# A decode attention block whose first 57 pairs run in a device loop of 19 rounds

## The chip, the cores and the metric

The kernel runs on one core of one Trainium2 chip. The metric is the device time of one execution in microseconds (us). A profile of one execution gives the instructions of each engine and the transfers of the DMA queues: PE does the matmuls (PEld their weight loads), DVE the vector work, ACT the activations, POOL next to nothing here, and SP issues nearly all transfers.

## What is computed

One token of each of two sequences goes through a pre-norm attention block with a cached history of 8192 keys and values for 32 heads of 128, and then through a dense block with a squared ReLU. All is float32. Cut to what matters:

```python
# x (2,1,512); k_cache, v_cache (2,32,8192,128); wq (512,4096); wo (4096,512)
q = (layernorm(x) @ wq).reshape(2, 1, 32, 128).transpose(0, 2, 1, 3)
scores = einsum("bhqd,bhkd->bhqk", q, k_cache) * 128 ** -0.5
o = einsum("bhqk,bhkd->bhqd", softmax(scores), v_cache)
h = x + o.transpose(0, 2, 1, 3).reshape(2, 1, 4096) @ wo
r = relu(layernorm(h) @ w1 + b1)          # w1 (512,1792)
out = h + (r * r) @ w2 + b2               # w2 (1792,512)
```

Keys and values are 537 MB, and the weights come to 24 MB more; each byte is used once.

## The kernel before

The work is cut into 64 pairs of a head and a sequence. A pair's keys and values lie side by side in one block of 128 partitions x 16384 numbers (8.39 MB), keys in the first half, values in the second. The tile `ring` has three such blocks, its slots. Pair i lies in slot (i + 1) modulo 3, except for the last two.

**Head.** SP loads the query weights into slot 0 (L69) and pairs 0 and 1 into slots 1 and 2 (L70, L71). The layer norm and the query projection run while these arrive (L127 to L146). L148 scales the 64 query columns and spreads each over 32 columns, which gives the tile QR. Pair 2 is loaded into slot 0 once the query weights have been read (L149).

**A pair.** `scores` (L157) does 32 matmuls of 128x512 on a score tile of four banks, of which the pool `psum` has two (line L162), and DVE takes the negated maximum of each row (L164). `exponentials` (L167) lets ACT do the exponential in place and add up the rows (L169). `weighted` (L171), four times a pair, lets DVE multiply the values by the exponentials and add up, in place in the slot (L174). The results of a pair go into column i of NM, LS and AC.

**Order of the work.** The loop at L236 over pairs 0 to 62 is a Python loop: its instructions stand one after the other in the program. After each pair SP gets the load of pair i + 3 into the slot just freed (L242, L58). SP's loads are one queue in order, and each waits until DVE is done with its slot. From pair 59 on, the output weights, halves of the last pairs and the two `group` steps (merging rows and projecting) are put in between (L243 to L258). After the loop come the weights of the dense block, the last pair and the tail (L260 to L341).

Of the kernel before, what the change touches and what calls it, by code (L numbers as in the profile page):

```python
# [8 lines left out]
F32 = mybir.dt.float32  # L9
AF = mybir.ActivationFunctionType  # L10
ALU = mybir.AluOpType
AX = mybir.AxisListType

B, H, SK, DH, D, F = 2, 32, 8192, 128, 512, 1792
P = 128
NQ = 4
CS = SK // NQ
NH = DH // 32
# [3 lines left out]
BH = H * B  # L22
ROW = 16384
HALF = ROW // 2
SLOTS = 3
BLK = 512
GROUPS = [(0, 16), (16, 31), (31, 32)]
W2_PIECES = [4, 4, 3, 2, 1]
EPS = 1e-5
SCALE = DH ** -0.5  # L30

# [2 lines left out]
def attention_block_kernel(ctx: ExitStack, tc: tile.TileContext, small, kvd, wqd, wod, w1d, w2d, out):  # L34
    nc = tc.nc
    consts = ctx.enter_context(tc.tile_pool(name="consts", bufs=1))
# [6 lines left out]
    def slot(i):  # L43
        return ring[:, (i + 1) % SLOTS if i < BH - 2 else i - BH + 3]

    def keys(i):
        return slot(i)[:, :HALF].rearrange("p (j c) -> p j c", j=NQ)

    def values(i):
        return slot(i)[:, HALF:].rearrange("p (e c) -> p e c", e=NH)  # L50
# [6 lines left out]
    def load_kv(i):  # L57
        nc.sync.dma_start(slot(i), kvd[i])  # L58

    def load_wo(a, b):  # L60
        nc.sync.dma_start(WO[:, a:b], wod[:, a:b])
# [14 lines left out]
    eps_t = consts.tile([P, 1], F32, name="eps_t")  # L76
    nc.vector.memset(eps_t, EPS)
    zero = consts.tile([P, 1], F32, name="zero")
# [11 lines left out]
    def banks(name="s"):  # L90
        t = psum.tile([P, NQ * BLK], F32, name=name)
        return t, [t[:, k * BLK : (k + 1) * BLK] for k in range(NQ)]

    def clear(ap, n):
        return nc.scalar.activation(ap, zero.to_broadcast([P, n]), AF.Copy)  # L95
# [27 lines left out]
    _, bk = banks()  # L123
# [11 lines left out]
    for k in range(2):  # L135
        for d in range(DB):
            for j in range(NQ):
                n = k * NQ + j
# [4 lines left out]
    for k in range(2):  # L143
        for m in range(NQ):
            at = k * BLK + m * DH
            nc.tensor.matmul(turned[:, k, m], big[:, at : at + DH], quads[:, :, :B], start=True, stop=True)  # L146
    QR = consts.tile([P, BH, 32], F32, name="QR")
    nc.vector.tensor_scalar(QR, bk[2][:, :BH, None].to_broadcast([P, BH, 32]), SCALE, None, op0=ALU.mult)  # L148
    load_kv(2)  # L149


    NM = consts.tile([P, BH], F32, name="NM")
    LS = consts.tile([P, BH], F32, name="LS")
    AC = consts.tile([P, BH, NH], F32, name="AC")
    OT = consts.tile([P, BH], F32, name="OT")

    def scores(i):  # L157

        s, bk = banks()
        for n in range(CS // BLK):  # L160
            for j in range(NQ):
                nc.tensor.matmul(bk[n][32 * j : 32 * j + 32, :], QR[:, i, :], keys(i)[:, j, n * BLK : (n + 1) * BLK],  # L162
                                 start=True, stop=True)
        nc.vector.tensor_reduce(NM[:, i : i + 1], s, axis=AX.X, op=ALU.max, negate=True)  # L164
        return s

    def exponentials(i, s):  # L167

        nc.scalar.activation(s, s, AF.Exp, bias=NM[:, i : i + 1], scale=1.0, accum_out=LS[:, i : i + 1])  # L169

    def weighted(i, s, e, lo, hi, acc, by=1.0):  # L171

        v = values(i)[:, e, lo:hi]
        return nc.vector.scalar_tensor_tensor(v, v, by, s[:, lo:hi], op0=ALU.mult, op1=ALU.mult, accum_out=acc)  # L174
# [44 lines left out]
    last = BH - 1  # L219
    g_at = [(a * B, b * B) for a, b in GROUPS]  # L220

    def group(n, project_now):

        a, b = g_at[n]
        _, bk = banks()
        w, rl = weigh(a, b, bk[0], bk[1])
        join(a, b, w, rl, bk[2])
        if project_now:
            clear(bk[3], D)
            add_rows(project(*GROUPS[n], bk[3]), bk[0])  # L230

    def load_half(i, half):
        cut = slice(half * HALF, (half + 1) * HALF)
        nc.sync.dma_start(slot(i)[:, cut], kvd[i][:, cut])

    for i in range(last):  # L236
        s = scores(i)
        exponentials(i, s)
        for e in range(NH):
            weighted(i, s, e, 0, CS, AC[:, i, e : e + 1])  # L240
        if i + 3 < last - 1:
            load_kv(i + 3)  # L242
        if i == last - 4:  # L243
            load_wo(0, H // 2)
        if i == last - 3:
            load_half(last - 1, 0)
            load_half(last - 1, 1)
            group(0, True)
        if i == last - 2:
            load_half(last, 0)  # L250
            load_wo(H // 2, H)
            for e in range(NH):
                n = 2 if e == NH - 1 else 1
                for k in range(n):
                    lo, hi = k * CS // n, (k + 1) * CS // n
                    at = HALF + e * CS
                    nc.sync.dma_start(values(last)[:, e, lo:hi], kvd[last][:, at + lo : at + hi])
            group(1, False)  # L258
# [3 lines left out]
    at = 0  # L262
    for n in W2_PIECES:
        nc.sync.dma_start(W2[:, at : at + n], w2d[:, at : at + n])
        at += n
    sl = scores(last)
    _, (hp, sums, y, o) = banks()
    y, o = y[:, :FQ], o[:, :P]
    clear(hp, D)
    clear(y, FQ)  # L270
    with tc.issue_after(clear(o, P).ins):
        exponentials(last, sl)
    a, b = g_at[2]
    w, rl = weigh(a, b, sums[:, :64], sums[:, 64:128])
    nc.scalar.activation(warm, w[:, 0:1], AF.Sqrt)
# [21 lines left out]
    for e in range(NH + 1):  # L297
        at = 32 * min(e, NH - 1)
# [73 lines left out]
```

## Time and profile before

| | before |
|---|---|
| median of 2 runs | 1309.41 us (1309.08 to 1309.75) |
| profiled execution | 1310.04 us, its span 1308.3 us |
| instructions | 6011 |
| PE busy | 417.7 us (32%) |
| DVE busy | 728.9 us (56%) |
| ACT busy | 145.0 us (11%) |
| moved by DMA | 561.44 MB, mean 429 GB/s |
| mean granted PE clock | 0.643 |

The span is the time from the first to the last instruction. "Busy" counts the time in which an engine executes, not its waits. A group of instructions is named by line, engine, operation and output<-input. In the chain that ended last, the profile goes back from the last instruction, at each step to what released it. In the waits, each line says which engine and line waited for what, how long in total, how often, and the longest.

### The profile page before, as it was taken

Reading aid. Unit: us, or ns where it says so; the run is one execution under the profiler, and the core shown is the slowest. Engines: PE = TensorE matmul, PEld = TensorE weight load, DVE = VectorE, ACT = ScalarE, POOL = GpSimd, SP = SyncE. Lnnn points to the kernel's source line nnn. Section 1 sums busy time; section 2 is a strip of 40 time slices with the busy share of each in tenths; the row PEclk is TensorE's granted clock in tenths of the full one; section 3 lists DMA queues with packets and bytes.
Section 4 is the critical chain, followed back from the end, with each engine's and each line's share of the span. In section 5 each row is a group of like instructions: output and inputs, shape, how many; then the busy total and the mean of one; then the engine's idle time right before and its main releaser. Section 6 shows DMA issues by size and latency. Waiting matters only on the chain.

```text
span 1308.3 us, 6011 instructions
## 1 busy us (share of the span) xinstructions
PE 417.7 (32%) x2438; PEld 114.7 (9%) x2438; DVE 728.9 (56%) x626; ACT 145.0 (11%) x152; POOL 0.7 (0%) x6
## 2 busy tenths in 40 slices
PE   2423223323323323322322332332332332332446
PEld 0100000000000000000000000000000000000113
DVE  0464665564565565565566466556456556556553
ACT  1111011011011011011101101101101101101111
POOL 0000000000000000000000000000000000000000
PEclk9666667566656666666656666756665665665766
DMA  9999999999999999999999999999999999999997
GB/s 417 417 447 425 439 433 431 441 425 443 425 439 423 441 429 435 433 435 432 433 431 435 430 437 431 435 431 433 431 437 429 437 429 437 428 439 429 426 426 313
DMA packets 12122, 561.44 MB, mean 429 GB/s; under 512 B 1472, under 2 KB 1600, under 8 KB 2752
## 3 DMA queue, kind: packets, MB, share of 16 engines
q1 hardware_dynamic: 11952, 561.06, 99.3%
q8 instruction: 19, 0.31, 0.1%
q14 instruction: 7, 0.06, 0.0%
q10 hardware_dynamic: 144, 0.01, 0.0%
HBM read 561.00 MB, written 0.07 MB: 429 GB/s over the span
## 4 chain that ended last, share of the span: by engine, by line
DMA 62%; DVE 20%; PE 12%; ACT 4%; another core or an unknown queue 1%; issue 1%; SPq 0%; ACTq 0%
DMA ring<-in_kvd 62%; DVE ring L174 16%; PE s L162 11%; DVE NM L164 4%; ACT s L169 4%; PE s L315 0%; PE s L337 0%; PE s L308 0%; DVE yT L329 0%; PE s L189 0%; PE s L321 0%; PE s L327 0%; SPq L58 0%; PE s L326 0%
## 5 line engine op out<-in xcount | busy, mean ns | idle before, releaser
L162 PE MATMUL s<-ring,QR 128*32 128x512 f32 x2048 | 373.1, 895 | 827.1 <-DMA ring<-in_kvd 718.9
L174 DVE SCALAR_TENSOR_TENSOR ring<-ring,s 128x2048 f32<-128x2048 f32 x252 | 561.5, 2284 | 133.6 <-ACT s L169 133.6
L164 DVE TENSOR_REDUCE NM<-s 128x1 f32<-128x2048 f32 x64 | 146.6, 2291 | 383.4 <-PE s L162 383.4
L169 ACT ACTIVATE s<-s,NM 128x2048 f32<-128x2048 f32 x64 | 124.3, 1942 | 1072.5 <-DVE NM L164 1072.5
L162 PEld LDWEIGHTS s<-ring,QR 128*32 128x32 f32 x2048 | 93.3, 156 | 1104.4 <-issue 1100.9
L174 DVE DVE_READ_ACCUMULATOR ring<-ring,s 128x1 f32 x252 | 20.9, 83 | 0.0
L99 DVE TENSOR_REDUCE part<-sm 128x2 f32<-128x8 f32 x1 | 0.2, 160 | 21.9 <-DMA sm<-in_small 21.9
L169 ACT ACTIVATION_READ_ACCUMULATOR s<-s,NM 128x1 f32 x64 | 12.3, 193 | 0.0
L139 PE MATMUL s<-ring,xn 128*2 128x512 f32 x64 | 9.5, 749 | 1.5 <-ACT rstd L117 0.8
L174 DVE SCALAR_TENSOR_TENSOR ring<-ring,w,s 128x2048 f32<-128x2048 f32 (+1 forms) x5 | 9.6, 1916 | 0.6 <-DMA ring<-in_kvd 0.4
L207 PE MATMUL s<-ring,OT 128*2 128x512 f32 x62 | 8.5, 682 | 3.8 <-DMA ring<-in_wod 3.5
L148 DVE TENSOR_SCALAR QR<-s 128x2048 f32<-128x2048 f32 x1 | 2.3, 2291 | 12.4 <-PE s L146 12.4
L104 PE MATMUL s<-part,ones_d 128*128 128x2 f32 x2 | 0.6, 348 | 23.2 <-DVE hT L132 23.2
L189 PE MATMUL s<-lw,pick_all 128*128 128x32 f32 (+2 forms) x6 | 1.9, 393 | 14.9 <-DVE lw L188 14.9
L315 PE MATMUL s<-ring,xc 128*2 128x448 f32 x32 | 6.3, 942 | 0.6 <-ACT rstd L117 0.4
L181 PE MATMUL s<-NM,pick 128*128 128x32 f32 (+2 forms) x24 | 4.0, 309 | 7.1 <-DVE hT L217 4.6
L95 ACT ACTIVATE s<-zero 128x512 f32<-128x512 f32 (+2 forms) x6 | 3.2, 538 | 19.8 <-DVE OT L201 10.7
L337 PE MATMUL s<-ring,a 128*2 128x128 f32 x112 | 4.7, 348 | 1.5 <-DVE a L334 1.5
L181 PEld LDWEIGHTS s<-NM,pick 128*128 128x128 f32 x24 | 3.7, 236 | 8.9 <-issue 8.9
L117 ACT ACTIVATE rstd<-s,eps_t 128x2 f32<-128x2 f32 x2 | 0.5, 262 | 32.1 <-PE s L128 20.0
L337 PEld LDWEIGHTS s<-ring,a 128*2 128x2 f32 x112 | 3.3, 107 | 3.1 <-DVE a L334 2.0
L340 DVE COPY res<-s 128x128 f32<-128x128 f32 x1 | 0.3, 292 | 4.9 <-PE s L337 4.9
(74 smaller groups left out, 45.3 us busy)
## 6 DMA issues: line engine op xcount, KB each, us to landing
ring<-in_kvd SPq DMA_DIRECT2D x3, 4096.0 KB, 32.4
ring<-in_wod SPq DMA_DIRECT2D x2, 4096.0 KB, 41.8
ring<-in_w1d SPq DMA_DIRECT2D x4, 896.0 KB, 20.3
ring<-in_kvd SPq DMA_DIRECT2D x3, 1024.0 KB, 38.2
ring<-in_w2d SPq DMA_DIRECT2D x2, 1024.0 KB, 16.2
ring<-in_kvd SPq DMA_DIRECT2D x2, 512.0 KB, 38.0
ring<-in_kvd SPq DMA_DIRECT2D x62, 38.8
ring<-in_w2d SPq DMA_DIRECT2D x1, 768.0 KB, 16.8
```

Of the source, the lines that this page charges most:

```text
L95: return nc.scalar.activation(ap, zero.to_broadcast([P, n]), AF.Copy)
L139: nc.tensor.matmul(bk[k][32 * j : 32 * j + B, :], xn[:, d, :], WQ[:, d, n * BLK : (n + 1) * BLK], start=(d == 0), stop=(d == DB - 1))
L148: nc.vector.tensor_scalar(QR, bk[2][:, :BH, None].to_broadcast([P, BH, 32]), SCALE, None, op0=ALU.mult)
L162: nc.tensor.matmul(bk[n][32 * j : 32 * j + 32, :], QR[:, i, :], keys(i)[:, j, n * BLK : (n + 1) * BLK], start=True, stop=True)
L164: nc.vector.tensor_reduce(NM[:, i : i + 1], s, axis=AX.X, op=ALU.max, negate=True)
L169: nc.scalar.activation(s, s, AF.Exp, bias=NM[:, i : i + 1], scale=1.0, accum_out=LS[:, i : i + 1])
L174: return nc.vector.scalar_tensor_tensor(v, v, by, s[:, lo:hi], op0=ALU.mult, op1=ALU.mult, accum_out=acc)
L181: nc.tensor.matmul(pn[:, j], pick[:, j, :], NM[:, a:b], start=True, stop=True)
L189: nc.tensor.matmul(pl[:, :nb], pick_all, lw, start=True, stop=True)
L207: nc.tensor.matmul(hp[32 * j : 32 * j + B, :], OT[:, h * B : (h + 1) * B], WO[:, h, :], start=(h - h0 < NQ), stop=(h1 - h <= NQ))
L315: mm = nc.tensor.matmul(y[32 * j : 32 * j + B, :], xc[:, d, :], W1[:, d, j * FQ : (j + 1) * FQ], start=(d == 0), stop=(d == DB - 1))
L337: nc.tensor.matmul(o[32 * j : 32 * j + B, :], a2[:, m, :], W2[:, m, j * P : (j + 1) * P], start=False, stop=(m == FB - 1))
```

## The change

Pairs 0 to 56 are worked on in a loop on the device, `tc.For_i` from 0 to 57 in steps of 3. The body does three pairs, each followed by the load of the pair three further on; the load's source address is taken from the loop's register, its slot is fixed. `iteration_sync="reg_based"` is the way in which rounds are kept in order: waits in the body compare with registers that go up in every round. `head_align_engines` puts the start of the body at the start of a block of code for all five engines, and `hint_engines=()` gives no hints for the branch back.

In the body the queries and results are in small tiles with fixed addresses (q3, nm3, ls3, ac3). DVE spreads the next three query columns into q3 after the third pair's maximum, and copies the three results into NM, LS and AC at the end of the round. QT holds the scaled queries without the spread, and QR is left for the last seven pairs. Pairs 57 to 62 and what follows stay as they were, but for the new arguments of `scores` and `exponentials`.

```diff
+LOOPED = 57
...
-    QR = consts.tile([P, BH, 32], F32, name="QR")
-    nc.vector.tensor_scalar(QR, bk[2][:, :BH, None].to_broadcast([P, BH, 32]), SCALE, None, op0=ALU.mult)
+    QT = consts.tile([P, BH], F32, name="QT")
+    nc.vector.tensor_scalar(QT, bk[2][:, :BH], SCALE, None, op0=ALU.mult)
+    QR = consts.tile([P, BH - LOOPED, 32], F32, name="QR")
+    nc.vector.tensor_copy(QR, QT[:, LOOPED:, None].to_broadcast([P, BH - LOOPED, 32]))
     load_kv(2)
...
-    def scores(i):
+    def scores(i, q, nm):
...
-    def exponentials(i, s):
+    def exponentials(s, nm, ls):
...
-    for i in range(last):
-        s = scores(i)
-        exponentials(i, s)
+    q3 = consts.tile([P, SLOTS, 32], F32, name="q3")
+    nm3 = consts.tile([P, SLOTS], F32, name="nm3")
+    ls3 = consts.tile([P, SLOTS], F32, name="ls3")
+    ac3 = consts.tile([P, SLOTS, NH], F32, name="ac3")
+
+    def spread(at):
+        nc.vector.tensor_scalar(q3, QT[:, at, None].to_broadcast([P, SLOTS, 32]), 1.0, None, op0=ALU.mult)
+
+    spread(slice(0, SLOTS))
+    engines = (nc.tensor.engine, nc.vector.engine, nc.scalar.engine, nc.gpsimd.engine, nc.sync.engine)
+    with tc.For_i(0, LOOPED, SLOTS, hint_engines=(), head_align_engines=engines, iteration_sync="reg_based") as i0:
+        now = bass.ds(i0, SLOTS)
+        for u in range(SLOTS):
+            nm, ls = nm3[:, u : u + 1], ls3[:, u : u + 1]
+            s = scores(u, q3[:, u, :], nm)
+            if u == SLOTS - 1:
+                spread(bass.ds(i0 + SLOTS, SLOTS))
+            exponentials(s, nm, ls)
+            for e in range(NH):
+                weighted(u, s, e, 0, CS, ac3[:, u, e : e + 1])
+            nc.sync.dma_start(slot(u), kvd[bass.ds(i0 + (SLOTS + u), 1)].rearrange("o p c -> p (o c)"))
+        for all_, three in ((NM, nm3), (LS, ls3), (AC, ac3)):
+            nc.vector.tensor_scalar(all_[:, now], three, 1.0, None, op0=ALU.mult)
+
+    for i in range(LOOPED, last):
+        nm, ls = NM[:, i : i + 1], LS[:, i : i + 1]
+        s = scores(i, QR[:, i - LOOPED, :], nm)
+        exponentials(s, nm, ls)
         for e in range(NH):
             weighted(i, s, e, 0, CS, AC[:, i, e : e + 1])
```

More of the change, by code (lines that the diff above doesn't have):

```diff
@@ L161, in scores @@
             for j in range(NQ):
-                nc.tensor.matmul(bk[n][32 * j : 32 * j + 32, :], QR[:, i, :], keys(i)[:, j, n * BLK : (n + 1) * BLK],
+                nc.tensor.matmul(bk[n][32 * j : 32 * j + 32, :], q, keys(i)[:, j, n * BLK : (n + 1) * BLK],
                                  start=True, stop=True)
-        nc.vector.tensor_reduce(NM[:, i : i + 1], s, axis=AX.X, op=ALU.max, negate=True)
+        nc.vector.tensor_reduce(nm, s, axis=AX.X, op=ALU.max, negate=True)
         return s
-    def exponentials(i, s):
-        nc.scalar.activation(s, s, AF.Exp, bias=NM[:, i : i + 1], scale=1.0, accum_out=LS[:, i : i + 1])
+    def exponentials(s, nm, ls):
+        nc.scalar.activation(s, s, AF.Exp, bias=nm, scale=1.0, accum_out=ls)
     def weighted(i, s, e, lo, hi, acc, by=1.0):
@@ L265, in attention_block_kernel @@
         at += n
-    sl = scores(last)
+    sl = scores(last, QR[:, last - LOOPED, :], NM[:, last : last + 1])
     _, (hp, sums, y, o) = banks()
@@ L271, in attention_block_kernel @@
     with tc.issue_after(clear(o, P).ins):
-        exponentials(last, sl)
+        exponentials(sl, NM[:, last : last + 1], LS[:, last : last + 1])
     a, b = g_at[2]
```

## The prediction

> **What bounds the kernel now.** I read the utilisation slices first, then the chain that ended last, then the waits of PE and of SP's queue, and last one pair of the chain in order of time. From the first part of the page and its queue and chain parts:
>
> ```profile
> span 1308.3 us, 6011 instructions
> DMA  9999999999999999999999999999999999999997
> q1 hardware_dynamic: 11952, 561.06, 99.3%
> q8 instruction: 19, 0.31, 0.1%
> DMA 62%; DVE 20%; PE 12%; ACT 4%; another core or an unknown queue 1%; issue 1%; SPq 0%; ACTq 0%
> ```
>
> The DMA row is full in all but the last slice, and one queue (SP's) moves 561.06 MB in 99.3% of the span. No compute engine is near that. DVE's 20% and PE's 12% of the chain are misleading: the chain alternates between a transfer and the pair that frees its slot, and both sides run at the same time. The waits say the same:
>
> ```profile
> PE s L162 <- DMA ring<-in_kvd: 718.9, 54, 14.5
> SPq L58 <- DVE ring L174: 1129.7, 59, 25.4
> ```
>
> PE idles for some 13 us a pair until a load lands, and SP idles until DVE has freed a slot. One pair and the load it releases, in the chain in order of time (start, length, what):
>
> ```profile
> 62.77 6.25 PE s L162 x32
> 69.01 0.02 issue
> 69.03 2.30 DVE NM L164
> 71.34 0.02 issue
> 71.36 0.02 ACTq L169
> 71.38 0.05 issue
> 71.43 2.07 ACT s L169 x2
> 73.49 0.02 issue
> 73.52 8.93 DVE ring L174 x8
> 82.45 0.02 SPq L58
> 82.47 0.03 issue
> 82.50 38.18 DMA ring<-in_kvd
> 120.69 0.14 issue
> 120.82 6.24 PE s L162 x32
> ```
>
> Load 1 lands at 62.63 (PE starts 0.14 later), and load 4 is issued at 82.50: **a pair holds its slot for 19.87 us**. The matmul starts of the next pairs give the landing times:
>
> ```profile
> 82.12 5.07 PE L162 MATMUL s<-ring,QR 128*32 128x512 f32 x32 [13.15 <-DMA ring<-in_kvd]
> 101.47 5.63 PE L162 MATMUL s<-ring,QR 128*32 128x512 f32 x32 [14.28 <-DMA ring<-in_kvd]
> ```
>
> Less 0.14, loads 2 and 3 land at 81.98 and 101.33: **one load of 8.39 MB takes 19.35 us**, 434 GB/s. Issue to landing is 38.18 us because the load waits 18.8 us behind the one before it. So there is always one load moving and one nearly always queued, and an issue may come 18.8 us late before the DMA engines run dry. This cover decides everything below.
>
> **The change, part by part.**
>
> *Head, before the loop.* One QR of 128x2048 (2.29 us, 38.87 to 41.16) becomes QT (64 columns), QR for seven pairs (224 columns) and one spread (96 columns). The nearest rows are 0.16 us for 128x8, 0.22 for 128x128 and 0.42 for 128x512; 0.2 + 0.3 + 0.2 = 0.7 us. The gain of 1.6 us lies under load 0, which lands at 42.02: 0.
>
> *In each of 19 rounds.* DVE gets one spread and three small copies, 0.2 + 3 x 0.16 = 0.7 us. It is busy 33.6 us in 58 (the window from 500 to 558), so it stays far from a bound. The spread stands behind the reduction of the third pair and ahead of its weighted sums, where DVE waits 2.12 us for ACT's exponential anyway, and needs PE to be done with q3, which the reduction has needed already. The copies come after a pair's last load is released: 0. SP's loads get an address from a register: 0.33 us for one issue before; were it 1 us, the 18.8 covers it: 0.
>
> *PSUM.* Three score tiles a round over two buffers: third pair and next round's first pair fall on the same buffer. PE must then wait for DVE's weighted sums. They end 19.87 after landing, and the next load lands at 19.35, so PE is held for 0.5 us once in three pairs, again under the cover: 0.
>
> *The branch.* PE has finished the third pair's matmuls 6.4 us after landing and would be idle for 13 us; DVE has 6.6 us between its last sum and the next reduction. Branch and register work of up to that length is not seen at all, and a first pair that is late by up to another 18.8 us is made up in the round, since three pairs keep DVE busy for 3 x (2.3 + 2.1 + 8.9) = 40 of 58 us: 0.
>
> *Code.* 54 pairs of 64 leave the instruction stream. The instruction queue's 0.31 MB takes at most 0.7 us at 434 GB/s: −0.6, the only gain that I see.
>
> *The two edges of the loop.* This is the step with a price, and the trace of before has no row for it. The body is written once, so its waits name the same semaphores in every round and compare with a register. In the first round no load of the body has happened yet: loads 0 to 2 were issued outside (L70, L71, L149). Either every engine settles ahead of the loop what its body needs from outside, or each wait of the body also covers the outside load of its own slot. At the end, the straight code for pairs 57 to 63 waits on fixed numbers again; either all that the loop has under way, loads 57 to 59 included, is settled before that code starts, or each of them is waited for singly. I bound each edge from both sides.
>
> Low end: single waits, 0 (a gain is excluded, since the DMA engines are full up to there). High end: all settled. **Entry:** PE starts pair 0 not at 42.16 but after load 2, at 81.98. No slot is free before 81.98 + 19.87 = 101.85, so the DMA engines, with nothing queued, stand still for one pair's time. A load started on an idle queue takes longer than one in a full queue; the only such row is the first weights' load:
>
> ```profile
> sm<-in_small ACTq DMA_DIRECT2D x1, 13.0 KB, 22.1
> ring<-in_wqd SPq DMA_DIRECT2D x1, 21.9
> ```
>
> 21.9 − 19.35 = 2.55 us for the restart. With 0.5 us for the engines to meet (0.8 is what DVE waited for the others at the program's start), load 3 lands at 101.85 + 0.5 + 21.9 = 124.25 instead of 101.33: **+22.9**. Afterwards loads 3, 4 and 5 are issued 13.3 us apart (DVE's pace) while each takes 19.35, so the queue fills again and nothing more is lost. **Exit:** pair 57 starts after load 59 instead of load 57; the same 19.87 + 2.55, and twice 0.75 us to meet and to start the code behind: **+23.9**. Pairs 58 and 59 then run ahead at 13.3 us, and the tail (the last loads, the second weights, 25 us after the last load) shifts as it is.
>
> I take the high end at both edges: a body with a single set of waits is nearest to settling everything outside it. What is late next is only the DMA stream as a whole, by 46.8 us.
>
> **Sum.** +22.9 + 23.9 − 0.6 = +46.2 on the profiled execution's 1310.04 (1308.3 span and 1.74 around it), 1356.2. That execution is 0.63 above the median of 1309.41, so about **1355.5**, +3.5%. Without restart and meeting costs it would be 2 x 19.87 − 0.6 = +39.1, 1348.5; with 5 us more at each edge 1365.
>
> **The rivals.**
>
> *Not slower: the edges wait load by load.* Then PE starts pair 0 at 42 and pair 57 on load 57, the queue never empties, and the sum is −0.6 plus perhaps 1: 1309 to 1310. For it: loads 0 to 2 have three separate landings that could be named singly. Against it: a wait inside the body has to be true in all 19 rounds. It decides if the idle stretch after load 2 is under 1 us. Chance 0.07.
>
> *One edge only.* Either edge settles all, the other waits singly: 1309.4 + 23 = 1332, +1.7%. Chance 0.09; more likely exit alone than entry alone.
>
> *The queue runs dry in every round.* If the back edge too let everything land, a round would last 19.87 for the first pair, 2.55 restart and 3 x 19.35 for three loads = 80.5 instead of 58.05: 18 x 22.4 = 403 more on top of the edges, 1758. Against it: the loop is asked for waits on registers, which would have no use if all were settled at each round's end. Chance 0.04.
>
> *The branch costs a code fetch.* The 13 KB load above needed 22.1 us beside a full queue; its 144 packets are nine on each of 16 engines, so one packet's turn is 2.4 us. A fetch of code is one packet of 16 KB (19 packets, 0.31 MB), so 2.4 us, and 22.1 at worst. Both are within PE's 13 us and the 18.8 us behind them; only beyond 32 us a round would it be paid, and 10 us beyond would add 18 x 10 = 180, 1535. Chance 0.03. The Trainium skill, Runtime: NRT & Kernel Launch, section Instruction fetch mechanics, says that a taken branch whose target is outside a window of two pages of 256 instructions stalls until the page is fetched, and that kernels therefore prefer full unrolling; by that rule a body of three pairs, with 192 weight loads and matmuls on PE, would still be within the window. No run of before has a branch that shows it.
>
> **How the numbers follow.** Both edges settled: 0.76, own range 1345 to 1368. The rivals take 0.07 + 0.09 + 0.04 + 0.03; 0.01 is left for a gain over 2%, which a full DMA row all but excludes. 2% (26 us) is about what a measurement here can tell from no change. Slower by more: 0.76 + 0.04 + 0.03, and 0.01 of the one-edge case, should its edge cost over 26: 0.84. Within 2%: 0.07 + 0.08 = 0.15. Faster: 0.01. The range reaches down to one edge, 1331, and up to 1372.
>
> **What would show it.** Right: the first matmul of L162 near 82 instead of 42; two stretches of some 20 us without DMA, one from 82 to 104 and one after load 59; between them rounds of 58.0 us with a full DMA row; pairs 1 and 2 at 13.3 us apart right after the entry. Wrong: the first score matmul at 42; DMA below full in the middle slices; rounds longer than 58.5 us.

## The result, and the profile after

The kernel with the loop takes 1369.03 us (median of 2 runs, 1366.49 to 1371.58), before 1309.41. The ratio is 1.0455, 95% interval 1.0371 to 1.054: slower by 3.7 to 5.4%. The forecast was 1355.5 and a range of 1331 to 1372. That the sum came out near is luck: one of its two edges cost nothing, and the rounds, which it had at nothing, cost 35 us.

From the page of the profiled execution (1371.58 us, of which the span is 1369.8):

```profile
span 1369.8 us, 6916 instructions
...
DMA  9999999999999999999999999999998989976997
...
q1 hardware_dynamic: 11952, 561.06, 95.8%
q8 instruction: 5, 0.08, 0.0%
```

The same 561.06 MB now fill 95.8% of a longer span: 57 us without SP's data, against 9 before (0.7% of 1308.3). These 48 us are not all of the 61.5 by which the span grew: the packets of the queue also took 13 us longer per engine. The row of tenths shows part of it late in the span; the rest is in slices that still read 9. The windows split it (start:end, length, then busy time of PE, PEld, DVE, ACT and POOL, granted clock, DMA share, GB/s):

```profile
100.00:500.00 400.00, 114.96 (x640) 29.00 (x640) 221.12 (x203) 50.15 (x47) 0.00 (x0) 0.63 0.98 420
500.00:900.00 400.00, 115.52 (x640) 29.19 (x640) 223.97 (x208) 50.15 (x47) 0.00 (x0) 0.62 0.97 416
...
1225.00:1245.00 20.00, 8.77 (x64) 2.44 (x64) 13.35 (x11) 5.31 (x5) 0.00 (x0) 0.76 0.00 1
```

The second of these stretches in the program before:

```profile
500.00:900.00 400.00, 119.56 (x652) 29.85 (x656) 233.13 (x188) 41.17 (x40) 0.00 (x0) 0.62 1.00 433
```

In the rounds the engines move 416 to 420 GB/s where the straight program moved 433, and there is one standstill, from 1225 to 1245, right behind the loop.

**The entry.** Starts of PE's matmuls:

```profile
43.64 5.56 PE L165 MATMUL s<-ring,q 128*32 128x512 f32 x32 [7.47 <-DMA ring<-in_kvd]
63.15 6.05 PE L165 MATMUL s<-ring,q 128*32 128x512 f32 x32 [13.95 <-issue]
82.45 4.93 PE L165 MATMUL s<-ring,q 128*32 128x512 f32 x32 [13.25 <-DMA ring<-in_kvd]
103.05 6.58 PE L165 MATMUL s<-ring,q 128*32 128x512 f32 x32 [15.66 <-DMA ring<-in_kvd]
```

Pair 0 starts at 43.64, when load 0 has landed, not at 82. The loop is entered with loads 1 and 2 under way.

**The rounds.** DVE's instructions of pairs 0 and 1 in the first round:

```profile
49.41 2.29 DVE L167 TENSOR_REDUCE nm<-s 128x1 f32<-128x2048 f32 x1 [12.32 <-PE s L165]
69.41 2.29 DVE L167 TENSOR_REDUCE nm<-s 128x1 f32<-128x2048 f32 x1 [17.71 <-PE s L165]
71.61 2.28 DVE L177 SCALAR_TENSOR_TENSOR ring<-ring,s 128x2048 f32<-128x2048 f32 x1
```

The maximum of pair 0 ends at 51.7, its exponential at 55.1, and its weighted sums do not start. DVE's queue has the maximum of pair 1 next, and that waits 17.71 us for load 1. In the source the sums of a pair stand ahead of the next pair's maximum, and in the program before they did so on the chip (pair 1, and the maximum of pair 2; the other sums of pair 1 stand between):

```profile
69.03 2.29 DVE L164 TENSOR_REDUCE NM<-s 128x1 f32<-128x2048 f32 x1 [7.20 <-PE s L162]
73.52 2.29 DVE L174 SCALAR_TENSOR_TENSOR ring<-ring,s 128x2048 f32<-128x2048 f32 x1 [2.19 <-ACT s L169]
...
87.25 2.29 DVE L164 TENSOR_REDUCE NM<-s 128x1 f32<-128x2048 f32 x1 [4.81 <-PE s L162]
```

In the body that was compiled from the same order of the source they do not; why is not known. So the slot of pair 0 is free only at 80.7, and SP issues load 3 then, 1.67 us before load 2 lands (82.40). I call this time the **cover** of a load: the landing of the load ahead, less its own issue. Before, it was 18.5 to 20.3 us. Over 18 rounds of the new kernel the first load has a mean cover of 1.99 us (1.4 to 2.9) and lands 1.96 us later than 19.35 us behind the load ahead (0.5 to 3.4); the second and third loads have 14.5 and 20.5 us and lose 0.0 and 0.2.

**The exit.** From the waits of SP and of PE:

```profile
SPq L249 <- DMA ring<-in_kvd: 37.8, 2, 19.3
...
PE s L165 <- PEq L395: 53.0, 1, 53.0
```

L249 is the loop. SP waits there for the last loads, and PE for 53 us until all engines go on: load 59 lands at 1224.33, PE starts pair 57 at 1225.10, load 60 is issued at 1245.13 and lands at 1267.03.

**The account** (landing times of both profiles): load 2 is 0.4 us later than before, load 59 35.8 later (1224.33 against 1188.57), load 60 59.1 later (1267.03 against 1207.92), the span 61.5. So rounds 35.3, exit 23.4, head 0.4, tail 2.4.

### The profile page after: what moved, and what is told of

It reads as the page before. It is cut to its first block, busy times and chain, and to the rows that moved or that the text cites. A ratio compares the mean times of both kernels' runs of the same rounds, so it can differ in the third digit from the quotient of the medians.

```text
span 1369.8 us, 6916 instructions
## 1 busy us (share of the span) xinstructions
PE 414.6 (30%) x2438; PEld 114.6 (8%) x2438; DVE 730.7 (53%) x704; ACT 169.5 (12%) x171; POOL 0.7 (0%) x6
## 3 DMA queue, kind: packets, MB, share of 16 engines
q1 hardware_dynamic: 11952, 561.06, 95.8%
## 5 line engine op out<-in xcount | busy, mean ns | idle before, releaser
L165 PE MATMUL s<-ring,q 128*32 128x512 f32 x1824 | 328.2, 885 | 807.8 <-DMA ring<-in_kvd 723.8
L167 DVE TENSOR_REDUCE nm<-s 128x1 f32<-128x2048 f32 x57 | 130.6, 2290 | 468.9 <-PE s L165 468.7
L172 ACT ACTIVATE s<-s,nm 128x2048 f32<-128x2048 f32 x57 | 110.7, 1942 | 643.1 <-DVE nm L167 642.9
L165 PEld LDWEIGHTS s<-ring,q 128*32 128x32 f32 x1824 | 82.6, 155 | 1052.5 <-issue 1038.3
L165 PE MATMUL s<-ring,QR 128*32 128x512 f32 x224 | 38.9, 860 | 88.9 <-PEq L395 53.0
L167 DVE TENSOR_REDUCE NM<-s 128x1 f32<-128x2048 f32 x7 | 16.0, 2291 | 64.4 <-PE s L165 64.4
L172 ACT ACTIVATE s<-s,NM 128x2048 f32<-128x2048 f32 x7 | 13.6, 1942 | 62.5 <-DVE NM L167 62.5
L165 PEld LDWEIGHTS s<-ring,QR 128*32 128x32 f32 x224 | 9.7, 151 | 116.1 <-issue 116.1
L210 PE MATMUL s<-ring,OT 128*2 128x512 f32 x62 | 11.4, 883 | 3.1 <-DMA ring<-in_wod 2.9
L172 ACT ACTIVATION_READ_ACCUMULATOR s<-s,nm 128x1 f32 x57 | 11.0, 193 | 0.0
## 6 DMA issues: line engine op xcount, KB each, us to landing
ring<-in_w1d SPq DMA_DIRECT2D x4, 896.0 KB, 20.3
```

The source lines that it names most:

```text
L165: nc.tensor.matmul(bk[n][32 * j : 32 * j + 32, :], q, keys(i)[:, j, n * BLK : (n + 1) * BLK], start=True, stop=True)
L167: nc.vector.tensor_reduce(nm, s, axis=AX.X, op=ALU.max, negate=True)
L172: nc.scalar.activation(s, s, AF.Exp, bias=nm, scale=1.0, accum_out=ls)
L210: nc.tensor.matmul(hp[32 * j : 32 * j + B, :], OT[:, h * B : (h + 1) * B], WO[:, h, :], start=(h - h0 < NQ), stop=(h1 - h <= NQ))
```

## The experiments

Theory A: the rounds' loss comes from DVE's order in the body, through the late issue of a round's first load. Theory B: it is the branch, the waits on registers or the shared score buffer. Theory C: the exit lets all loads land and costs a pair's time, the restart and the meeting. Theory D: the second loss belongs to the tail, whatever comes before it.

### The order put back in the loop

```diff
-        nc.vector.tensor_reduce(nm, s, axis=AX.X, op=ALU.max, negate=True)
+        with (tc.issue_after(behind.ins) if behind else ExitStack()):
+            nc.vector.tensor_reduce(nm, s, axis=AX.X, op=ALU.max, negate=True)
...
-            s = scores(u, q3[:, u, :], nm)
+            s = scores(u, q3[:, u, :], nm, done if u else None)
...
-                weighted(u, s, e, 0, CS, ac3[:, u, e : e + 1])
+                done = weighted(u, s, e, 0, CS, ac3[:, u, e : e + 1])
```

> The loop as it is, with each pair's maximum on VectorE queued behind the weighted sums of the pair before it. Theory A (the order on VectorE in the body, maximum of pair 1 ahead of the sums of pair 0, issues the first load of a round 18 us late and eats the cover): rounds of 58.1 to 58.3 us instead of 60.2, so 18 x 1.94 = 35 us less, about 1334. Theory B (the branch, the waits on registers or the score buffer shared by two rounds cost 1.94 us a round): rounds stay at 60.2, about 1369.

Measured: 1330.72 us, ratio 1.0177 (1.016 to 1.0194). Rounds take 58.12 us, and cover is 17.2 us or more everywhere. The windows of the rounds and of the stretch behind the loop:

```profile
100.00:500.00 400.00, 117.55 (x672) 29.56 (x672) 232.25 (x212) 52.20 (x49) 0.00 (x0) 0.65 1.00 433
500.00:900.00 400.00, 114.79 (x664) 29.18 (x668) 235.47 (x214) 50.14 (x47) 0.00 (x0) 0.64 1.00 434
...
1187.00:1206.00 19.00, 8.04 (x64) 2.16 (x56) 13.19 (x9) 4.70 (x5) 0.00 (x0) 0.77 0.00 1
```

The rounds run at the full rate again, with the branch, the registers and the shared buffer still in them: theory B falls. One more thing is in them that nobody had counted: both loops load ACT's table once a round (ACT_TABLE_LOAD, 1.28 us), between the first pair's maximum and its exponential, and in the rounds before there was no such load. DVE waits 3.5 us there in the ordered loop instead of 2.1 to 2.2. That costs cover, which is 17.2 to 17.4 us from the second round on, and no time. What is left is the exit: load 59 lands at 1185.73, load 60 is issued at 1206.30 and lands at 1228.25.

### The order alone, without a loop

```diff
-        s = scores(i)
-        exponentials(i, s)
-        for e in range(NH):
-            weighted(i, s, e, 0, CS, AC[:, i, e : e + 1])
+        if i < LOOPED and i % SLOTS == 0:
+            s, _ = scores(i)
+            exponentials(i, s)
+            ahead, red = scores(i + 1)
+            exponentials(i + 1, ahead)
+            with tc.issue_after(red.ins):
+                for e in range(NH):
+                    done = weighted(i, s, e, 0, CS, AC[:, i, e : e + 1])
...
```

(the second pair's sums follow, and the third pair as before, each held behind the last sum)

> The straight program of before, no loop, with VectorE held to the order that the loop's body has for pairs 0 to 56. Theory A: three pairs take about 60.2 us instead of 58.3, 19 x 1.9 = 36 us more, about 1345. Theory B: nothing is lost without a branch, 1309.

Measured: 1350.79 us (1342.13 to 1360.02 over 4 runs), ratio 1.0305 (1.0237 to 1.0373). Rounds take 60.9 us, the first load's cover is 2.22 us, its mean loss 2.37. The order by itself, in a program without a loop, costs what the rounds of the loop cost, here 42 us.

### How much cover is needed

The same straight program, but with one, two or three of the first pair's four sums ahead of the second pair's maximum:

```diff
+            for e in range(FIRST):
+                done = weighted(i, s, e, 0, CS, AC[:, i, e : e + 1])
-            ahead, red = scores(i + 1)
+            ahead, red = scores(i + 1, done)
             exponentials(i + 1, ahead)
             with tc.issue_after(red.ins):
-                for e in range(NH):
+                for e in range(FIRST, NH):
```

> The straight program, with two of the first pair's four sums on VectorE ahead of the second pair's maximum and two behind it: the round's first load is then issued some 6 us before the load ahead of it lands (before: 18.8, with the loop's order: 1.5). Theory A1 (only a cover below the restart of 2.55 us costs): as before, 1309. Theory A2 (the 16 DMA engines end a load at different times, so a short cover already lets some of them run dry): part of the 42 us that the loop's order costs, 1315 to 1340.

> The same with three sums ahead and one behind: some 8.4 us of cover. Theory A1: 1309. Theory A2: less than with two ahead, 1309 to 1325.

> The straight program, with one of the first pair's four sums on VectorE ahead of the second pair's maximum and three behind it: some 4.5 us of cover for the round's first load, between the 6.6 that cost nothing and the 2.2 that cost 2.4 us a round. If the edge lies at the restart of 2.55 us: 1309. If it lies nearer to 6: 1315 to 1340.

| sums ahead | cover of the first load, mean | loss of the first load, mean | time | ratio, interval |
|---|---|---|---|---|
| 0 | 2.22 us | 2.37 us | 1350.79 | 1.0305 (1.0237 to 1.0373) |
| 1 | 4.78 us | 0.19 us | 1314.57 | 1.0044 (1.0027 to 1.0061) |
| 2 | 6.64 us | 0.08 us | 1308.51 | 1.0 (0.9991 to 1.001) |
| 3 | 8.56 us | 0.10 us | 1308.22 | 0.9995 (0.9986 to 1.0005) |
| 4 (before) | 19.44 us | 0.09 us | 1308.46 | 1 |

Each ratio is to the program before as it ran alongside (1308.61, 1308.88 and 1308.46 us).

Two sums ahead cost nothing, so a cover of 6.6 us is as good as 19. At a mean of 4.8 us single loads are late: three with a cover of 3.8 to 4.0 us by 0.4 to 1.4 us, while one with 3.6 us is not. (Load 18 is 0.66 us late with 4.8 us and load 57 1.24 us with 5.0 us, but no engine stood idle ahead of them; load 18 is late with 19.7 us too, by 0.38.) At 2 us nearly all are. The restart of 2.55 us is not the edge (theory A1 misses there). By single loads the edge lies near 4 us, by the time between means of 4.8 and 6.6 us.

Theory A2 gave a wrong time, since two sums cost nothing, but the packets in the traces show its cause. A packet of 65536 bytes takes 2.42 us, and the 16 engines do not end a load together: in the rounds of the new kernel the last engine ended 0.5 to 3.2 us behind the first. The first packet of such a load starts about 1 us behind its issue at the earliest. So with 2 us of cover the engines that end early stand idle, 1.39 us each on average at the first load of a round (26 us over 19 rounds), and the packets then take up to 3.9 us (12 us more per engine in these loads). With one sum ahead the idle time is 0.09 us, with two or more none.

### The loads cut in two inside the body, DVE's order left as compiled

```diff
+            nxt = kvd[bass.ds(i0 + (SLOTS + u), 1)].rearrange("o p c -> p (o c)")
+            nc.sync.dma_start(slot(u)[:, :HALF], nxt[:, :HALF])
             exponentials(s, nm, ls)
...
-            nc.sync.dma_start(slot(u), kvd[bass.ds(i0 + (SLOTS + u), 1)].rearrange("o p c -> p (o c)"))
+            nc.sync.dma_start(slot(u)[:, HALF:], nxt[:, HALF:])
```

> The changed kernel with its own order on VectorE, but in the body each load is cut in two: the keys' half is issued once PE has read the keys, the values' half after the sums. Theory A (what costs is the late issue, not the order itself): 9.7 us of data are queued in time, rounds of 58.1 to 58.4, about 1331 to 1336. Rival (the order delays the compute itself): rounds of 60.2, about 1369.

Measured: 1335.67 us, ratio 1.0206 (1.0189 to 1.0223). The first pair's keys have been read 6 us after landing, whatever DVE does. With their half queued early, the poor order is left in place and the rounds' loss is gone. Rounds take 58.3 us. So it is the late issue that costs, not the order as such. A load in two halves takes 19.43 us instead of 19.35, which makes some 4 of the 5 us over the ordered loop.

### The loop left twice

```diff
+SPLIT = 30
...
-    with tc.For_i(0, LOOPED, SLOTS, ...
+    for first, end in ((0, SPLIT), (SPLIT, LOOPED)):
+        with tc.For_i(first, end, SLOTS, ...
```

> The ordered loop, cut into two loops of 10 and 9 rounds, so that a loop is left twice. Theory C (leaving a loop lets all loads land and costs one pair's time, the restart and the meeting, 23 to 26 us each time): the ordered loop's time plus 25, about 1359. Rival D (the second loss lies in the tail after pair 57, whatever comes before it): the same time as the ordered loop, about 1334.

Measured: 1358.75 us, ratio 1.0382 (1.0364 to 1.0399), 28 us over the ordered loop. In the middle load 32 lands at 662.70, load 33 is issued at 685.87 and lands at 707.65, 25.6 us more than the usual 19.35; the rest of the difference in span (28.5) comes mostly after the last weights' landing (5.8 us to the end instead of 3.5). Theory D falls, and C holds: each loop that is left costs one standstill.

### A first piece freed early behind the loop

```diff
+    done = None
     for i in range(LOOPED, last):
...
-        s = scores(i, QR[:, i - LOOPED, :], nm)
+        s = scores(i, QR[:, i - LOOPED, :], nm, done)
+        if i + 3 < last - 1:
+            load_half(i + 3, 0)
         exponentials(s, nm, ls)
...
         if i + 3 < last - 1:
-            load_kv(i + 3)
+            load_half(i + 3, 1)
```

> The ordered loop; after it, pairs 60 and 61 are loaded by halves, the keys' half as soon as PE has read the keys of pairs 57 and 58, and VectorE is held to the pairs' order there too. Theory C (the DMA engines stand still until a first piece of a slot is free): the standstill after the loop falls from 20 to 6.5 us, so 13 us less than the ordered loop, about 1321. Rival D, or a standstill set by the meeting of the engines: the same as the ordered loop, about 1334.

Measured: 1325.99 us, ratio 1.0133 (1.0116 to 1.015): 4.7 us less than the ordered loop, not 13. At the exit it does what was forecast: the first half is issued at 1192.41, against 1206.30 for the whole load. The end shows where the gain went:

```profile
1300.00:1309.00 9.00, 5.65 (x40) 3.72 (x44) 5.16 (x14) 0.00 (x0) 0.00 (x0) 0.73 0.99 407
1310.00:1318.00 8.00, 6.09 (x150) 4.08 (x146) 1.42 (x6) 0.26 (x1) 0.00 (x0) 0.94 0.01 4
```

The last weights land at 1310.85, 13.9 us earlier than in the ordered loop (1324.79), and the span ends 10.0 us later, not 3.5: the last pairs' work now ends after the last transfer. (The profiled execution was the shortest of four, so it shows 7.4 of the 13.9; by the medians 4.7 are kept.) Theory C stands, but behind a standstill the tail has only a few us before it sets the end itself.

### A barrier in every round

```diff
-    ... iteration_sync="reg_based") as i0:
+    ... iteration_sync="barrier") as i0:
```

in the ordered loop.

> The ordered loop with iteration_sync set to barrier. If the barrier lets all loads land in every round: a round is 19.9 for the first pair, 2.55 restart and 58.05 for three loads, 80.5, and 1 to 2 for the barrier; 19 x (81.5 - 58.1) over the straight program, about 1754. If it stops only the engines and leaves loads under way: a few us over the ordered loop, about 1340 to 1370.

Measured once: 1744.5 us. Two windows of its trace, the start of a round and a whole round:

```profile
141.00:161.00 20.00, 9.94 (x64) 2.66 (x64) 10.84 (x8) 3.34 (x3) 0.00 (x0) 0.67 0.00 0
303.00:384.00 81.00, 15.70 (x96) 4.13 (x96) 33.90 (x31) 7.57 (x8) 0.00 (x0) 0.56 0.73 311
```

PE starts a round at 303.20 and the next at 384.08, 80.9 us, and the DMA engines stand still for its first 20. The forecast's rival of a queue that runs dry in each round (80.5 us a round) is what this form of the loop does. The form on record does not.

None of these versions beats the straight program; the best of them without a loop (three sums first) is the same.

## Why the prediction was right or wrong

The time fell into the range, but two of the prediction's own three signs of being wrong came: the first score matmul started at 43.64, and rounds took 60.2 us. Its mechanism was right for the bound and the exit, and wrong for the entry and the rounds.

**The bound** was right. The kernel is set by the loads, each standstill of the DMA engines shows in full, and the work on DVE, the copies, the branch and the address from a register cost nothing: the ordered loop has them all and runs its rounds in 58.12 us.

**"I take the high end at both edges"** failed for the entry: forecast +22.9, measured 0.4. Of the two possibilities named, the profile shows what the second would give: PE starts pair by pair as loads 0, 1 and 2 land. The argument that a body with one set of waits is nearest to settling everything outside it was no evidence. A second, fixed wait could stand beside the one on a register and be true in every later round; whether the body is made so is not shown.

**The exit** was right: +23.9 forecast, +23.4 measured (20.80 from landing to issue, of which 0.77 is the meeting, and 21.90 to landing, less 19.35). Two loops showed a second standstill, 25.6 us. The row of the first weights' load, 21.9 us on an idle queue, was the right price for the restart.

**"A first pair that is late by up to another 18.8 us is made up in the round: 0"** is the step that cost most. The cover was read correctly from the trace of before. What was wrong was to take DVE's order in the body to be that of the source, sums ahead of the next maximum. The order on the chip used up the cover by itself, 37.2 us from landing to issue instead of 19.87, and 18 rounds at 1.96 us are 35. The statement that an issue may come 18.8 us late for free is also too generous: 6.6 us of cover were enough and 4.8 were not quite, so some 12 are free.

**Code**, forecast −0.6. The rounds of the ordered loop gain about 2.8: load 59 lands at 1185.73 in the ordered loop, 1188.57 before. In the trace of before, six loads of 54 took longer than 19.43 us, together 3.5 us more; five of the seven small fetches of 8 KB after the start (383.5, 616.7, 869.3 and 1121.8 us, and one at 365.4) lie in or beside the four longest of these gaps, 0.4 to 0.97 us each. A packet of data that starts 0.3 to 0.4 us behind each of these four takes 3.1 us instead of 2.42. From the second round on the ordered loop has no fetch up to load 59, and no load is late. That the fetch causes the delay was not tried by itself. The Trainium skill, Runtime: NRT & Kernel Launch, section Instruction fetch mechanics, says that a boundary of code costs one step of a fetch queue and is mostly hidden. Most of the 15 fetches of 16 KB up to load 59 in the program before agree: twelve fall into loads that are not late and two into loads 0.1 and 0.2 us late. The first, at 46.1, falls into load 1, which took 20.61 us, and the four of 8 KB do not agree.

**The rivals.** "One edge only" was right on the edges, and its 1332 is what the ordered loop measured, 1330.72. It did not have the second loss, and so its time was not the kernel's. The code fetch at each branch, with 0.03, did not happen: the trace of the new kernel has no fetch of code between 47.4 and 1227.8 us, so all but the first of its rounds are free of them.

The total was within 14 us because +22.9 that did not come stood against +35.3 that nobody had counted. That is luck: had the entry cost what was forecast, the kernel would have taken some 1391 us, outside of the range.

## What to carry to other kernels

In a kernel set by its loads, work out for each load how long before the landing of the load ahead it is issued, and read it again in the trace after any change: here 6.6 us cost nothing, 4.8 cost 0.4%, 2 cost 3%. The body of this loop was compiled into another order than the same source without a loop, so look at the order of each engine's instructions before blaming the branch, and pin the one that frees a buffer. This loop on the device, with waits on registers, was entered with loads in flight, but leaving it emptied the queue and cost a pair's time once; a barrier paid that in every round.

## What was not expected of the hardware

A load that is issued 1.4 to 2.9 us before the load ahead of it lands still ends 0.5 to 3.4 us late, and by no fixed relation: a cover of 2.25 us cost 3.23, one of 2.47 cost 0.57. The landing is that of the last of 16 engines, and how far apart they end changes from load to load (0.5 to 3.2 us), so that an engine's idle time can show at a later load (load 6: engines idle for 0.55 us on average, 3.23 late; load 9: 1.74 and 1.24). A load on a quite empty queue needs 21.9 us instead of 19.35; there the first packets start 1.0 to 1.8 us behind the issue and take 2.5 to 3.5 us instead of 2.42. So 2.55 is what one would expect to lose at most without any cover. Why the landing of some loads was later than that, by up to 3.4 us, is left open in part: the packets show idle engines and longer packets, and what makes those packets longer was not tried.
